# Masks later, fewer tile-mode changes, and the last gate tile in two column halves

## The chip, the cores and the metric

The kernel runs on one core of one Trainium2 chip. The metric is device time in microseconds, the median of seven runs. The profile is that of one execution, taken by the hardware profiler; TensorE is called PE in it, its weight loads PEld, VectorE DVE, ScalarE ACT, GpSimd POOL and SyncE SP. L977 is line 977 of the kernel before.

## The reference, cut to what matters

One sequence of S = 2048 tokens with D = 448 features goes through a linear attention with 16 heads of 28 features and through a squared-ReLU network of F = 1792 hidden units; the second gates the first.

```
xn = layernorm(x)
q, k, v = split(xn @ wqkv)                 # 16 heads of 28
phi(t) = where(t > 0, t + 1, exp(t)) + 1e-6
kv = sum over tokens of phi(k) v^T         # per head, 28 x 28
z  = sum over tokens of phi(k)             # per head, 28
s  = (phi(q) kv / (phi(q) z + 1e-6)) @ wo
g  = silu(relu(xn @ w1 + b1)^2 @ w2 + b2)
out = x + s * g
```

All inputs and the output are bf16.

## The kernel before, in words

The tokens are 16 tiles of 128 (NT); four tiles are a group of 512 (NG = 4). D = 448 is contracted as three chunks of 128 features and a tail of 64. The transposed tile xT holds the tail twice, on partitions 0 to 63 and 64 to 127 (the copies `dup`, L713, and L495 double these columns of xn ahead of the transposition), and the weight tiles hold their 64 tail rows twice as well. So a tail of one product can run on the upper half of the TensorE array while that of another runs on the lower.

A "mode" is how the array is cut into tiles for a matmul: 128x128 (rows x columns) is the whole array, 64x128 two row halves side by side, 128x64 two column halves. The mode follows from the partitions of the operands and of the output.

**Who sets the order.** The kernel is written as a list of operations (`Program.add`), each with its engine, what it reads and writes, and an assumed duration. `schedule()` keeps TensorE and SyncE in the order of the source and lets the other engines choose, by assumed times, the ready operation that is due first. `prio`, `rank` and `hold` change that choice. `emit()` derives the semaphore waits from the reads and writes. An engine executes its list in order, so an operation that waits holds all behind it. `Buf` names a PSUM bank, and eight exist.

**Stages**, in TensorE's order:
1. The start (L1108 to L1145): `warm` issues 43 matmuls on a zero tile. Beside it tiles 0 to 3 are loaded and normalised one by one (`ln_stats`, `ln_rstd`, `ln_norm`, `dup`), and TensorE transposes them (`x_transpose0`, L726; two tiles at a time, evicted by ACT and DVE). The first eight H products (`hh`) are worked off in column halves as the tiles arrive (`pe_part`, L701). `bias_columns` transposes b1 (L780). POOL makes the constants: `ident`, and the masks `hmask`, `zmask` and `ehd` by twelve `affine_select` operations on the memset tiles (`late_constants`, L383).
2. The middle (L1154 to L1182): K, Q and H products of the groups in fours (`quads`, `pe_four`), in 64x128 mode. Later tiles are transposed by DMA. `phi` (L598) evicts K and Q by ACT (exp) and two DVE operations; `h_out` (L670) evicts H by ACT and squares it on DVE or ACT. `qx` (L653) forms the last 64 q features of eight tiles. `zsum` (L628) adds the k tiles on POOL. Four gate tiles (`gg`, L967) are already made here.
3. Attention sums (L1176 to L1181): `token_sum` contracts xn with phi(k) over all tokens; `z_cols` (L840) turns zb, the sum on each partition, into the vector z by five one-column matmuls, and DVE spreads it with `zmask` into zsb; `den` forms phi(q) z.
4. The rest: `spread` brings 1/den to all features with `ehd` and multiplies it into phi(q); `fold_wv` and `fold_wo` form kv wo, with `hmask`. Then gate tiles (`ggs`) alternate with S tiles (`ss4`). A gate tile is 14 matmuls of 448 columns (L977), an addition of b2 on DVE (L994) and a silu on ACT (L1004). An S tile is multiplied by its gate tile on DVE (L1014), x is added on POOL (L1020), and SP issues the output.
5. The end (L1206 to L1219): gate tiles 13 and 14; the tails of S tiles 12 to 15 (`s_tails`, tile 15 as 256 and 192 columns); the other chunks (`s_main`) of tiles 12 and 13; 11 of the 14 matmuls of gate tile 15, led by b2 as a one-row matmul (L975); tile 14; the last three gate matmuls; the two parts of tile 15. Gate tile 15 is read by silu straight from PSUM (L989). Here x is added on DVE. SP waits for all outputs at the very end.

Of the kernel before, what the change touches and what calls it, by code (L numbers as in the profile page):

```python
# [6 lines left out]
ALU = mybir.AluOpType  # L7
AF = mybir.ActivationFunctionType

P = 128  # L10
S, D, F = 2048, 448, 1792
NT, NG, NF = S // 128, S // 512, F // 128
NH, DH = 16, 28
# [281 lines left out]
def bass_recurrent_scan__linear_attn_block__dense_activation_squared_relu__prompt_kernel(  # L295
    nc, A_x, A_wqkv, A_wo, B_x, B_w1, B_b1, B_w2, B_b2, out
):
    with ExitStack() as es:
# [11 lines left out]
        onesr = sb("onesr", [1, P], bf)  # L310
        ehd = sb("ehd", [P, D], bf)
        x_tok = sb("x_tok", [P, NT, D], bf)
        xn = sb("xn", [P, NT, 512], bf)
# [17 lines left out]
        zb = sb("zb", [P, D], bf)  # L331
# [23 lines left out]
        def select(view, name, pattern, base, cm, fill, op=ALU.is_ge, dur=0.3):  # L355
            masks.append(
                add(
                    "pool",
                    lambda e, _: e.affine_select(
                        out=view, in_=view, pattern=pattern, compare_op=op, fill=fill, base=base, channel_multiplier=cm  # L360
                    ),
                    [name], [name], dur,
                )
            )

        masks = []
# [8 lines left out]
        vset(onesr[:, :], 1.0, "onesr")  # L375
        vset(zsb[:, :, :], 0.0, "zsb0")
# [3 lines left out]
        vset(kvm[:, :, :], 0.0, "kvm", dur=1.0)  # L380
        pool(lambda e, _: e.memset(eps6[:, :], 1e-6), ["eps6"], dur=0.1)

        def late_constants():  # L383
            hv = hmask[:, :].rearrange("p (b j) -> p b j", b=HC)
            select(hv, "hmask", [[-DH, HC], [0, DH]], 0, 1, 0.0)
            select(hv, "hmask", [[DH, HC], [0, DH]], DH - 1, -1, 0.0)
            for view, pat, base in (
                (zmask[:, 0:3, :], [[P, 3], [-DH, 32]], 0),
                (zmask[:, 3, :], [[-DH, 32]], 384),
                (zmask[:, 4, :], [[-DH, 32]], 320),  # L390
            ):
                select(view, "zmask", pat, base, 1, 0.0)
                select(view, "zmask", [[-a, n] for a, n in pat], DH - 1 - base, -1, 0.0)
            select(zmask[:, 3, :], "zmask", [[0, 32]], 63, -1, 0.0)
            select(zmask[:, 4, :], "zmask", [[0, 32]], -64, 1, 0.0)
            pool(lambda e, _: e.memset(ones[:, :], 1.0), ["ones"], dur=0.1)
            ev = ehd[:, :].rearrange("p (h j) -> p h j", h=NH)
            for g in range(NG):
                select(ev, "ehd", [[-1, NH], [0, DH]], -32 * g, 1, 1.0, ALU.not_equal, dur=0.6)
# [62 lines left out]
        masks.clear()  # L462
        late_constants()
# [164 lines left out]
        def zsum(i):  # L628
            o = zb if i == NT - 1 else zacc
            add(  # L630
                "pool",
                lambda e, _: e.tensor_tensor(  # L632
                    out=o[:, :], in0=pk[:, 0, :] if i == 1 else zacc[:, :], in1=pk[:, i, :], op=ALU.add
                ),
                [("pk", i), ("pk", 0) if i == 1 else "zacc"], ["zb" if i == NT - 1 else "zacc"], 1.05,
            )

# [15 lines left out]
        def qx(u):  # L653
            b = Buf("QX")

            def f(e, _):
                last = None
                for c in range(4):
                    rw = slice(0, 128) if c < 3 else slice(0, 64)
                    for o in (0, 1):  # L660
                        last = e.matmul(  # L661
                            ps(b)[64 * o : 64 * o + 64, 0:512], w_qkv[rw, c, 384:448],
                            xT[rw, 8 * u + o : 8 * u + 8 : 2, c, :], start=(c == 0), stop=(c == 3),
                        )
                return last

            add("pe", f, xnames(2 * u) + xnames(2 * u + 1) + wnames("wq"), [b], 4 * MM(512) + 0.1)
            phi(b, pqx[:, u, :, :].rearrange("p a b -> p (a b)"), ("pqx", u), 512)
# [171 lines left out]
        def z_cols():  # L840
            b = Buf("Z")

            def f(e, _):
                last = None
                for c in range(3):
                    last = e.matmul(
                        ps(b)[:, c : c + 1], zb[:, c * P : (c + 1) * P], ones[:, :], start=(c == 0), stop=True,
                        skip_group_check=True,
                    )
                for o in (0, 1):  # L850
                    last = e.matmul(
                        ps(b)[64 * o : 64 * o + 64, 3 + o : 4 + o], zb[:, 384:448], ones[:, :], start=False, stop=True,
                        skip_group_check=True,
                    )
                return last

            add("pe", f, ["zb", "ones"], [b], 0.35)
            for v, c0, c1, lo, hi in ((0, 0, 3, 0, 128), (1, 3, 4, 0, 64), (2, 4, 5, 64, 128)):

                def zops(e, _, c0=c0, c1=c1, lo=lo, hi=hi):  # L860
                    z = ps(b)[lo:hi, c0:c1]
                    z = free_ap(z, [[1, c1 - c0], [0, 32]])
                    return e.tensor_tensor(out=zsb[lo:hi, c0:c1, :], in0=z, in1=zmask[lo:hi, c0:c1, :], op=ALU.mult)

                add("dve", zops, [b, "zmask", "zsb0"], [("zsb", v)], 0.2)

# [28 lines left out]
        def den():  # L895
            def f(e, _):
# [19 lines left out]
                [("zsb", v) for v in range(3)] + [("pq", g, c) for g in range(NG) for c in range(3)]  # L916
# [50 lines left out]
        def gg(si, b=None, part=None):  # L967
            b = b or Buf("G")
            g = si // 4
            fis = range(NF) if part is None else part  # L970

            def f(e, _):
                last = None
                if part is not None and fis[0] == 0:
                    last = e.matmul(ps(b)[:, 0:D], onesr[:, :], b2b[0:1, :], start=True, stop=False)  # L975
                for fi in fis:
                    last = e.matmul(  # L977
                        ps(b)[:, 0:D], r2[:, fi, si * P : (si + 1) * P], w_2[:, fi, :],
                        start=(fi == 0 and part is None), stop=(fi == NF - 1),
                    )  # L980
                return last

            rd = [("r2", g, fi) for fi in fis] + ["w2"] + (["b2b", "onesr"] if part is not None else [])
            add("pe", f, rd + ([b] if fis[0] else []), [b], len(fis) * MM(D) + (0.19 if part is not None else 0))
            gs = gbuf[:, si % NGB, :]
            if part is not None:
                if fis[-1] == NF - 1:
                    add(
                        "act", lambda e, _: e.activation(out=gs, in_=ps(b)[:, 0:D], func=AF.Silu), [b, "acts"],  # L989
                        [("g", si % NGB)], 0.576,  # L990
                    )
            else:
                add(
                    "dve", lambda e, _: e.tensor_tensor(out=gs, in0=ps(b)[:, 0:D], in1=b2b[:, :], op=ALU.add),  # L994
                    [b, "b2b"], [("g", si % NGB)], 0.624,
                )
# [11 lines left out]
        def gate(si, b, lo, hi, k, final):  # L1008
            w = hi - lo
            gs, ob = gbuf[:, si % NGB, lo:hi], obuf[:, si % NOB, lo:hi]  # L1010
            nm = ("o", si % NOB)
            wr = [nm] if k is None else [("ol", k)] + ([nm] if lo == 0 else [])
            add(
                "dve", lambda e, _: e.tensor_tensor(out=ob, in0=ps(b)[:, 0:w], in1=gs, op=ALU.mult),  # L1014
                [b, ("g", si % NGB)], wr, 0.1 + w * 0.00118,
            )
            nm = wr[0]
            add(
                "dve" if final else "pool",
                lambda e, _: e.tensor_tensor(out=ob, in0=ob, in1=x_tok[:, si, lo:hi], op=ALU.add),  # L1020
                [nm, ("x", si)], [nm], 0.08 + w * 0.0007 if final else 1.05,
            )
            dma("sp", tok(out, si, si + 1)[:, 0, lo:hi], ob, [("out", si, lo)], P * w * 2, [nm])
# [84 lines left out]
        warm(43, 0.106)  # L1108
# [24 lines left out]
        for op in masks:  # L1133
            op.hold = [t23]
# [15 lines left out]
        ln(4, 8, lead=3, hold=[t23])  # L1150
        load_x(12, 16)
# [17 lines left out]
        gg(3)  # L1169
        quads("H2.8 H2.9 H2.10 H2.11 Q1.1 H2.12 Q1.2 H2.13")  # L1170
# [40 lines left out]
        us = s_tails([(12, 0, D), (13, 0, D), (14, 0, D), (15, 0, 256), (15, 256, D)])  # L1211
        s_main(us[0], 0)
        s_main(us[1], 1)
        gb = Buf("G")
        gg(15, gb, range(0, 11))
        s_main(us[2], 2)
        gg(15, gb, range(11, NF))
        s_main(us[3], 3)
        s_main(us[4], 4)  # L1219
# [30 lines left out]
```

## Time and profile before

| | us |
|---|---|
| median of seven runs | 148.54 (148.14 to 148.94) |
| the profiled execution | 148.76 |
| its span | 147.0 |
| first warm-up matmul starts | 1.05 |
| first transpose starts | 5.80 |
| last matmul starts | 143.40 |
| last output issued | 144.97 |

The profiled execution took 148.76 us; its span, from the first to the last instruction that the profiler recorded, is 147.0, so 1.7 us lie around it. The views used below are: the page's first section (busy time, share of the span and number of instructions of each engine); the chain that ended last, followed back from the end through whatever released each step, as shares and as a list in order of time; the timeline, one row for consecutive instructions of one kind, with the idle time before them and what ended it in brackets; and the DMA issues with their time to landing. [...] consecutive matmuls overlap: the distance between their starts is what one costs.

### The profile page before, as it was taken

What the parts mean: (1) busy time and instruction counts of PE and PEld (TensorE: products, weight loads), DVE (VectorE), ACT (ScalarE), POOL (GpSimd) and SP (SyncE); (2) the same over time, 40 slices, a digit from 0 to 9 for tenths busy, and PEclk for the clock granted to TensorE, in tenths of its full rate; (3) what the DMA queues carried; (4) which work ended last, traced back from release to release, by engine and by line L of the source; (5) the groups of instructions that cost most, each with busy time, mean ns of one, the idle gap of its engine ahead of it and who ended that gap; (6) DMA issues with size and microseconds to landing.
All of it is one profiled execution on the core that took longest, in us unless ns stands there. A gap on an engine that the chain in (4) does not pass through costs nothing.

```text
span 147.0 us, 2838 instructions
## 1 busy us (share of the span) xinstructions
PE 142.2 (97%) x1127; PEld 72.7 (49%) x1127; DVE 97.2 (66%) x222; ACT 79.3 (54%) x152; POOL 34.4 (23%) x50
## 2 busy tenths in 40 slices
PE   7999999999999999999999999999999999999990
PEld 7874555555454444444443554454444545545450
DVE  6979699799987995268999410079674426136343
ACT  3618797988886981388879713897311110310200
POOL 6800025371000551000550000000001908109100
PEclk9999999999999999999999999999999999999999
DMA  3967799933900600000000000000000211102212
GB/s 85 322 224 229 162 236 381 304 102 62 85 0 18 124 4 0 0 0 4 2 0 0 4 0 0 0 7 0 0 0 0 71 58 61 64 0 65 64 62 62
DMA packets 16025, 10.53 MB, mean 72 GB/s; under 512 B 7372, under 2 KB 15628, under 8 KB 16012
## 3 DMA queue, kind: packets, MB, share of 16 engines
q1 hardware_dynamic: 15824, 10.28, 26.8%
q8 instruction: 9, 0.15, 0.5%
q10 hardware_dynamic: 188, 0.07, 0.2%
q14 instruction: 4, 0.03, 0.1%
HBM read 6.94 MB, written 1.84 MB: 60 GB/s over the span
## 4 chain that ended last, share of the span: by engine, by line
PE 94%; ACT 3%; DVE 1%; issue 0%; DVEq 0%
PE pb L977 29%; PE pb L705 25%; PE pb L622 7%; PE pb L793 6%; PE pb L646 6%; PE pb L1031 6%; PE pb L1081 3%; PE pb L701 2%; ACT r L672 2%; PE pb L661 2%; PE pb L1067 1%; PE pb L799 1%; PE pb L878 1%; PE pb L737 1%; PE pb L938 1%; PE pb L822 1%
## 5 line engine op out<-in xcount | busy, mean ns | idle before, releaser
L977 PE MATMUL pb<-w,r 128*128 128x448 bf16 x224 | 44.3, 353 | 0.0
L672 ACT ACTIVATE r<-pb,b1f 128x512 bf16<-128x512 f32 x54 | 33.8, 690 | 10.6 <-PE pb L705 10.6
L705 PE MATMUL pb<-xT,w 64*128 64x512 bf16 (+1 forms) x291 | 38.7, 377 | 0.3 <-ACT r L672 0.3
L977 PEld LDWEIGHTS pb<-w,r 128*128 128x128 bf16 x224 | 21.1, 98 | 21.2 <-issue 2.0
L1004 ACT ACTIVATE gbuf<-gbuf 128x448 bf16<-128x448 bf16 x15 | 8.5, 580 | 29.7 <-DVE gbuf L994 29.7
L632 POOL TENSOR_TENSOR zacc<-zacc,pk 128x448 f32<-128x448 f32 x13 | 14.5, 1114 | 39.9 <-DVE pk L612 35.8
L1020 POOL TENSOR_TENSOR obuf<-obuf,x_tok 128x448 bf16<-128x448 bf16 x12 | 12.0, 1030 | 48.7 <-DVE obuf L1014 48.7
L705 PEld LDWEIGHTS pb<-xT,w 64*128 64x128 bf16 (+1 forms) x291 | 15.0, 94 | 16.2 <-ACT r L672 0.7
L994 DVE TENSOR_TENSOR gbuf<-pb,b2b 128x448 bf16<-128x448 f32 x15 | 9.4, 624 | 16.6 <-PE pb L977 16.5
L686 DVE TENSOR_TENSOR r<-r 128x512 bf16<-128x512 bf16 x35 | 16.6, 512 | 3.0 <-ACT r L672 3.0
L1014 DVE TENSOR_TENSOR obuf<-pb,gbuf 128x448 bf16<-128x448 f32 (+2 forms) x17 | 9.2, 591 | 7.1 <-PE pb L1031 4.7
L622 PE MATMUL pb<-w_qkv,xT 64*128 64x448 bf16 x112 | 13.3, 350 | 0.0
L961 DVE TENSOR_TENSOR pqT<-pqT,pb 128x512 bf16<-128x512 bf16 x12 | 7.4, 680 | 8.6 <-PE pb L938 8.6
L687 ACT ACTIVATE r<-r 128x512 bf16<-128x512 bf16 x21 | 12.6, 634 | 0.0
L646 PE MATMUL pb<-xT,w_qkv 64*128 64x512 bf16 x84 | 11.1, 376 | 0.0
L705 PE MATMUL pb<-xT,w_1r 64*128 64x512 bf16 x56 | 10.5, 377 | 0.0
L612 DVE SCALAR_TENSOR_TENSOR pk<-pb,pk 128x448 bf16<-128x448 f32 x16 | 9.9, 624 | 0.5
L600 ACT ACTIVATE pk<-pb 128x448 bf16<-128x448 f32 x16 | 7.8, 541 | 4.4 <-PE pb L622 4.4
L466 DVE BATCH_NORM_STATS2 st<-x_tok 128x6 f32<-128x448 bf16 x16 | 9.2, 614 | 0.6 <-DMA x_tok<-in_A_x_dram 0.6
L793 PE MATMUL pb<-pk,xn 128*128 128x448 bf16 x48 | 9.4, 353 | 0.0
L622 PEld LDWEIGHTS pb<-w_qkv,xT 64*128 64x128 bf16 x112 | 5.8, 94 | 5.7 <-issue 0.4
L612 DVE SCALAR_TENSOR_TENSOR pqT<-pb,pqT 128x512 bf16<-128x512 f32 x12 | 8.2, 689 | 0.3
(90 smaller groups left out, 129.2 us busy)
## 6 DMA issues: line engine op xcount, KB each, us to landing
out_dram<-obuf SPq DMA_DIRECT2D x15, 112.0 KB, 1.8
w<-in_B_w_dram SPq DMA_DIRECT2D x1, 1568.0 KB, 9.5
x_tok<-in_A_x_dram SPq DMA_DIRECT2D x3, 448.0 KB, 4.0
w<-in_B_w_dram SPq DMA_DIRECT2D x3, 384.0 KB, 4.3
w_qkv<-in_A_wqkv_dram SPq DMA_DIRECT2D x3, 336.0 KB, 4.8
w_o<-in_A_wo_dram SPq DMA_DIRECT2D x1, 392.0 KB, 9.3
w_qkv<-in_A_wqkv_dram SPq DMA_DIRECT2D x6, 56.0 KB, 4.3
x_tok<-in_A_x_dram SPq DMA_DIRECT2D x2, 112.0 KB, 2.1
```

The costliest lines, as they stand in the source:

```text
L612: lambda e, _: e.scalar_tensor_tensor(out=slot, in0=ps(buf)[:, 0:n], scalar=1.0 + 1e-6, in1=slot, op0=ALU.add, op1=ALU.max),
L622: return e.matmul(ps(b)[:, 0:D], xT[rw, si, c, :], w_qkv[rw, c, D : 2 * D], start=start, stop=stop)
L632: lambda e, _: e.tensor_tensor(out=o[:, :], in0=pk[:, 0, :] if i == 1 else zacc[:, :], in1=pk[:, i, :], op=ALU.add),
L646: return e.matmul(ps(b)[:, 0:512], w_qkv[rw, c, m * P : (m + 1) * P], xT[rw, 4 * g : 4 * g + 4, c, :], start=start, stop=stop,)
L672: rl = lambda e, _: e.activation(out=slot, in_=ps(b)[:, 0:512], func=AF.Relu, bias=b1f[:, fi : fi + 1])
L686: return e.tensor_tensor(out=slot, in0=slot, in1=slot, op=ALU.mult)
L687: return e.activation(out=slot, in_=slot, func=AF.Square)
L705: return e.matmul(ps(b)[:, 0:512], lhs, xT[rw, 4 * g : 4 * g + 4, c, :], start=start, stop=stop, skip_group_check=not full,)
L793: last = e.matmul(ps(b)[:, 0:D], xn[:, si, c * P : (c + 1) * P], pk[:, si, :], start=(si == 0), stop=(si == NT - 1),)
L977: last = e.matmul(ps(b)[:, 0:D], r2[:, fi, si * P : (si + 1) * P], w_2[:, fi, :], start=(fi == 0 and part is None), stop=(fi == NF - 1),)
L994: "dve", lambda e, _: e.tensor_tensor(out=gs, in0=ps(b)[:, 0:D], in1=b2b[:, :], op=ALU.add),
L1020: lambda e, _: e.tensor_tensor(out=ob, in0=ob, in1=x_tok[:, si, lo:hi], op=ALU.add),
```

## The change

- **Masks.** `late_constants` is split. `z_masks` is called behind the LayerNorm of tiles 4 to 7, and its selects read the last transposed copy of tiles 2 and 3. `head_masks` (hmask and ehd) is called behind gate tile 3, and its selects read that tile. The small tile `ones` is set at the start as before. The memsets of `onesr` and of zsb go.
- **qx.** The tail chunk is no longer contracted on 64 rows but on all 128, where the features stand twice, with a new weight tile wqh = 0.5 x the doubled weights. DVE makes wqh once, from the loaded q weights, and qx reads it.
- **z_cols.** zb is widened to 512 columns, the last 64 a copy of its features 384 to 447 made by POOL behind the last `zsum`. The five one-column matmuls all use 128 weight columns, and one DVE operation writes all of zsb instead of three.
- **The end.** `s_tails` and the outputs cut tile 15 into 224 and 224 columns. The order is S tiles 12, 13, 14; the left half of gate tile 15 (`gg_part`: b2 by a matmul with `ident`, then 14 of 224 columns, silu of 224 columns from PSUM); the left half of S; the right half of the gate tile; the right half of S.
- **Warm-up.** 40 matmuls instead of 43.

In DVE's new order, wqh stands behind the second ReLU (L677) of the first group and ahead of the two squares (L686) that start at 15.51 in the profile. On POOL, the six head masks stand behind the eleventh `zsum`. TensorE's order is otherwise the same.

```diff
-        zb = sb("zb", [P, D], bf)
+        wqh = sb("wqh", [P, 64], bf)
+        zb = sb("zb", [P, 512], bf)
...
-        vset(onesr[:, :], 1.0, "onesr")
-        vset(zsb[:, :, :], 0.0, "zsb0")
...
-        def late_constants():
+        def z_masks(after):
...
+        def head_masks(after):
...
+            if i == NT - 1:
+                pool(lambda e, _: e.tensor_copy(zb[:, D:512], zb[:, 384:D]), ["zbd"], ["zb"], dur=0.25)
...
-                    rw = slice(0, 128) if c < 3 else slice(0, 64)
                     for o in (0, 1):
                         last = e.matmul(
-                            ps(b)[64 * o : 64 * o + 64, 0:512], w_qkv[rw, c, 384:448],
-                            xT[rw, 8 * u + o : 8 * u + 8 : 2, c, :], start=(c == 0), stop=(c == 3),
+                            ps(b)[64 * o : 64 * o + 64, 0:512], w_qkv[:, c, 384:448] if c < 3 else wqh[:, :],
+                            xT[:, 8 * u + o : 8 * u + 8 : 2, c, :], start=(c == 0), stop=(c == 3),
                         )
...
+            if u == 0:
+                add(
+                    "dve",
+                    lambda e, _: e.tensor_scalar(
+                        out=wqh[:, :], in0=w_qkv[:, 3, 384:448], scalar1=0.5, scalar2=None, op0=ALU.mult
+                    ),
+                    wnames("wq"), ["wqh"], 0.1,
+                )
...
-                for c in range(3):
+                for c in range(5):
+                    k = min(c, 3) * P
                     last = e.matmul(
-                        ps(b)[:, c : c + 1], zb[:, c * P : (c + 1) * P], ones[:, :], start=(c == 0), stop=True,
+                        ps(b)[:, c : c + 1], zb[:, k : k + P], ones[:, :], start=(c == 0), stop=True,
                         skip_group_check=True,
                     )
-                for o in (0, 1):
-                    last = e.matmul(
-                        ps(b)[64 * o : 64 * o + 64, 3 + o : 4 + o], zb[:, 384:448], ones[:, :], start=False, stop=True,
-                        skip_group_check=True,
-                    )
...
+        def gg_part(si, lo, hi):
+            b = Buf("G")
+            w = hi - lo
+
+            def f(e, _):
+                last = e.matmul(ps(b)[:, 0:w], ident[:, :], b2b[:, lo:hi], start=True, stop=False)
+                for fi in range(NF):
+                    last = e.matmul(
+                        ps(b)[:, 0:w], r2[:, fi, si * P : (si + 1) * P], w_2[:, fi, lo:hi], start=False,
+                        stop=(fi == NF - 1),
+                    )
+                return last
+
+            rd = [("r2", si // 4, fi) for fi in range(NF)] + ["w2", "b2b", "ident"]
+            add("pe", f, rd, [b], (NF + 1) * max(MM(w), 0.098))
+            add(
+                "act",
+                lambda e, _: e.activation(out=gbuf[:, si % NGB, lo:hi], in_=ps(b)[:, 0:w], func=AF.Silu),
+                [b, "acts"], [("gh", lo)] + ([("g", si % NGB)] if lo == 0 else []), 0.2 + 0.00084 * w,
+            )
...
-        warm(43, 0.106)
+        warm(40, 0.107)
...
         ln(4, 8, lead=3, hold=[t23])
+        z_masks([("xTp", 2, 3)])
...
         gg(3)
+        head_masks([("g", 3)])
...
-        us = s_tails([(12, 0, D), (13, 0, D), (14, 0, D), (15, 0, 256), (15, 256, D)])
-        s_main(us[0], 0)
-        s_main(us[1], 1)
-        gb = Buf("G")
-        gg(15, gb, range(0, 11))
-        s_main(us[2], 2)
-        gg(15, gb, range(11, NF))
-        s_main(us[3], 3)
-        s_main(us[4], 4)
+        us = s_tails([(12, 0, D), (13, 0, D), (14, 0, D), (15, 0, 224), (15, 224, D)])
+        for k in range(3):
+            s_main(us[k], k)
+        gg_part(15, 0, 224)
+        s_main(us[3], 3)
+        gg_part(15, 224, D)
+        s_main(us[4], 4)
```

## The prediction

> **What bounds the kernel now.** I read the page's busy times first, then the share line of the chain that ended last, then that chain in order of time, and last the timeline of the few places that the change touches.
>
> ```profile
> PE 142.2 (97%) x1127; PEld 72.7 (49%) x1127; DVE 97.2 (66%) x222; ACT 79.3 (54%) x152; POOL 34.4 (23%) x50
> ...
> PE 94%; ACT 3%; DVE 1%; issue 0%; DVEq 0%
> ```
>
> TensorE has work in 97% of the span and is 94% of the chain. So an edit pays in one of three ways: it takes time out of TensorE's stream, it shortens what runs before TensorE has its data (the first 6 us), or what runs after its last matmul (the last 4 us). Work of other engines in between is worth nothing until it makes TensorE wait. The chain by time (start us, duration us, what) shows all places:
>
> ```profile
> 1.05 4.71 PE pb L1081 x43
> 5.76 0.11 PE pb L780
> 5.87 0.70 PE pb L737 x8
> ...
> 38.05 1.10 PE pb L661 x8
> ...
> 86.90 0.05 PE pb L846 x3
> 86.95 0.12 PE pb L851 x2
> 87.08 3.13 PE pb L793 x16
> ...
> 97.24 2.65 PE pb L977 x14
> ...
> 104.85 2.75 PE pb L977 x14
> ...
> 139.45 0.29 PE pb L975
> 139.74 2.19 PE pb L977 x11
> ...
> 143.10 0.55 ACT gbuf L989
> 143.68 0.69 DVE obuf L1014 x2
> 144.37 0.20 DVE obuf L1020
> ```
>
> Price of one tile-mode change: the 14 matmuls of a gate tile take 2.65 us behind another full-array group (97.24; 0.189 us each) and 2.75 us behind a group of 32-row tiles (104.85): 0.10 us. The eight matmuls of qx (L661) take 1.10 us where eight q matmuls in one mode take 0.86 us elsewhere in the chain: two changes, 0.12 us each. So 0.10 to 0.12 us a change, and it is TensorE's own time.
>
> **Part 1, mode changes.** qx before runs six matmuls as 128x64 tiles, then two as 64x64; with wqh all eight are 128x64. One change less, twice in the kernel: 2 x 0.11 = 0.22 us (bounds 0.20 and 0.24). z_cols before is three full matmuls, two of 128x64, and back to full: 0.05 + 0.12 us and the surplus of the 16 after it (3.13 against 16 x 0.189 = 3.03), together 0.27. After, five full ones: 0.05 for three and about 0.03 for each further one, 0.11. Saved 0.16 us; if a one-column matmul with a 128-column weight cost 0.06 each, as the 16 at L822 do (0.96 us), still 0.05. I take 0.15.
>
> These edits hang work on other engines. zb's copied columns are one small POOL copy behind the last zsum, which ends at 75.9 us, 10.8 us ahead of z_cols: nothing. Three DVE operations on zsb become one; den reads it 3 us later: nothing. wqh is a new DVE operation with a new wait, for the three loads of the q weights, and in DVE's order it stands ahead of two squares:
>
> ```profile
> 15.51 0.75 DVE L686 TENSOR_TENSOR r<-r 128x512 bf16<-128x512 bf16 x2
> 17.42 0.28 DVE L605 TENSOR_SCALAR pk<-pk 128x448 bf16<-128x448 bf16 x1 [1.16 <-ACT pk L600]
> ```
>
> The last of the loads is issued at 12.56 and takes 3.8 us, so it lands at 16.4. DVE then holds the two squares from 15.5 to 16.4, runs wqh (0.1 to 0.2) and the squares (0.75) and is free at 17.3 to 17.4. Its next work waits for ScalarE until 17.42 anyway. The idle 1.16 us covers it, with 0.1 us to spare. Without that cover, the pk operations behind it, and then the PSUM banks of the k tiles, would come free later, up to 0.2 us; TensorE has no wait there now, so I put it at 0, bounds 0 and +0.1.
>
> **Part 2, masks.** Before, POOL cuts twelve masks from 1.6 to 7.6 us, beside the LayerNorm chain of the first tiles:
>
> ```profile
> 3.82 3.17 POOL L359 TENSOR_SCALAR_AFFINE_SELECT ehd<-ehd 128x448 bf16<-128x448 bf16 x4
> ...
> 4.84 0.53 DVE L722 COPY xn<-xn 128x64 bf16<-128x64 bf16 x1
> ...
> 5.27 0.38 DVE L486 TENSOR_SCALAR xn<-x_tok,mv,rstd 128x448 bf16<-128x448 bf16 x1
> ...
> 7.89 0.18 DVE L722 COPY xn<-xn 128x64 bf16<-128x64 bf16 x1
> ```
>
> The same copy takes 0.18 us once POOL is quiet (7.89) and 0.53 at 4.84; it ends at 5.37, just behind the select that POOL ran from 4.62 to 5.33. So POOL's select held it. With the masks elsewhere the copy ends about 5.02 and the second normalisation starts when its rstd is there (ScalarE's row 4.89, 0.20: so 5.13) instead of 5.27. At its usual 0.38 it ends near 5.51, and the transposes can start at 5.56 to 5.58; before, they started at 5.80. The two memsets of zsb and onesr (0.1 to 0.2 us on DVE) were hidden: DVE waits 0.26 us for x at 2.96 anyway.
>
> The transposes at 5.80 were not only late for that: the 43 warm-up matmuls (0.107 each) ended there. Forty end 0.32 us earlier, at about 5.5 with the bias transpose. So trimming and masks only pay together, and the later of the two decides: 0.22 us, bounds 0 (the copy stays slow) and 0.32 (the whole trim). What is late next: the w1 block of the first H matmuls lands at 6.5 (issued 2.19, 4.3 us), 0.3 us before L701 starts at 6.79; its first matmul would then start at 6.57. The shift fits, just. Behind that DVE, ScalarE and TensorE follow one another in a chain with no slack until 15.2, so the 0.22 carries on.
>
> Here a rule speaks against the trim. The Trainium skill ("TensorE: Matmul & The Clock Gate", Part 1) says that the array runs at half rate until it has been busy through about one free-running window of 3.4 us. The trace agrees on the half rate (0.107 us per 128-column warm-up matmul, 0.056 per transpose from 5.87 on), and shows the release near 5.6, though the granted clock is printed as 1.00 throughout. By the row nothing is lost, since the release comes as the transposes start; by the rule a pause before the release could cost a second window. I take the row, as the pause is about 0.1 us, and keep the rule as the rival that ends slower.
>
> Where the masks go: the eight zmask selects (2.3 us) wait for the copy of xTp (2,3), so run from 10.3 to 12.6, beside statistics, which took 0.61 us with or without POOL, and end before the normalisations at 13.4. The four of ehd and two of hmask (3.8 us) wait for the fourth gate tile, which DVE adds at 58.8, so run to 63.3. POOL's next zsum starts at 69.6, DVE is idle for 2.58 us up to 62.0, and ehd and hmask are read behind 95. At worst two squares there are held 0.5 us, and nobody reads them for 40 us: 0.
>
> **Part 3, the end.** Before: the bias row as a one-row matmul (a change in, a change out: 0.29 + 2.19 against 12 x 0.189 = 2.27, 0.21 us too much), 14 gate matmuls, the two parts of the last S tile. Then a chain behind TensorE: silu of 448 columns, two multiplies, two adds, and an issue at 144.97 that is followed by 1.6 us to landing and 0.5 us to the end.
>
> After: 9 S matmuls from 138.14 (9 x 0.19, to 139.85), 15 gate matmuls of 224 columns, 3 of S, 15, 3. Spacing is linear in the columns (0.189 at 448; the six last, three of 256 and three of 192, start from 142.90 to 143.40: 0.109 and 0.083), so 0.096 at 224. Left half done at 141.29, S at 141.58, right half at 143.02, S at 143.31: the stream ends 0.17 us earlier than 143.48 (0.21 of mode changes, less 0.04 for 15 more instructions). The last gate matmul starts at 142.93 and is out 0.26 later, 143.19 (before 143.06). Silu +0.04; 224 columns cost about 0.35 (448 took 0.54; exp rows of 448 and 512 differ by 0.9 ns a column), to 143.57. Multiply +0.03, 0.385 (0.42 at 256, 0.35 at 192): 143.99. Add +0.03, 0.27: 144.29. Issue 144.32. All of the left half is over before 142.7 and its issue does not stand in front. Against 144.97: 0.65 us.
>
> A rule speaks against this too: the same page, section "LDWEIGHTS", gives columns / 1.2 ns, so 107 ns for 128 columns. Were that the pace, 30 narrow matmuls at 0.107 instead of 0.096 would cost 0.33 us. The row says no: with 192 columns, each with its own 128x128 load, they start every 0.083 us, and transposes every 0.056. I take the row; the rule makes the end 0.32 instead of 0.65.
>
> **The sum.** 0.22 + 0.15 + 0.22 + 0.65 = 1.24 us. The profiled execution took 148.76 us (span 147.0, 1.7 around it), so 147.52; it lies 0.22 above the median of the seven runs, 148.54, which gives 147.3.
>
> **The rivals.**
> - The start gives nothing: the copy is slow for another reason, or the first weights land later, and TensorE idles through the trimmed 0.32. For: the slack of w1 is 0.3 us. Against: the copy ends with POOL's select. 148.54 - 1.02 = 147.5.
> - The halves are paced by weight loads: 147.3 + 0.33 = 147.65. Against: the 0.083 row.
> - Slower: the pause before the clock's release costs another half-rate window. Place: 5.6 to 9.0 us, where TensorE is busy for 3.1 us (18 matmuls of 0.109, 16 transposes, 4 warm-ups); doubled, less what DVE hides, about +2 us: 147.5 + 2 = 149.5. It decides as soon as the 0.1 us of idle counts as a quiet window. Against: 4.5 of the first 4.6 us stay busy.
> - Slower too, by DVE held at wqh, needs the q weights 2 us later than they landed.
>
> **How the numbers follow.** All parts pay, 147.3: 0.66. No gain at the start, 147.5: 0.14. Weight-bound halves, 147.65: 0.08. Clock released late, 149.5: 0.07. Another new stall that eats it all: 0.05. 0.3% is 0.45 us, about what a measurement of this kernel can tell from no change: faster is below 148.1. The first three nearly all fall there: faster 0.82, same 0.09, slower 0.09. Range: all bounds good give 148.54 - (0.24 + 0.16 + 0.32 + 0.65) = 147.2; all bounds bad, weight-bound halves among them, 148.54 - (0.20 + 0.05 + 0 + 0.32) + 0.1 for DVE = 148.1. Below I add 0.3 for the runs' own spread (148.14 to 148.94): 146.9 to 148.1; the two slow cases, 0.12, lie outside.
>
> **What would show it.** The copy of dup at 0.18 and transposes near 5.58; qx 0.98 us in the chain; L793 behind z_cols at 3.03; the last output's issue near 143.7 (144.32 less the 0.59 won before it); gate matmuls every 0.096. Wrong if warm-up spacing of 0.107 goes on into L701, if DVE shows a wait on w_qkv beyond 17.4, or if silu of 224 columns takes nearly 0.54.

## The result and the profile after

| | before | after |
|---|---|---|
| median, us | 148.54 (148.12 to 149.29, 31 runs) | 147.24 (146.86 to 147.93, 12 runs) |
| profiled execution, us | 148.76 | 147.93 |
| its span, us | 147.0 | 146.2 |

The ratio is 0.9915, with a 95% interval of 0.9898 to 0.9933: 1.3 us faster. The prediction was 147.3. The profiled execution is the longest of the twelve, and its span is only 0.8 us shorter than that of before; why is part of what follows.

The page of the changed kernel, busy times and shares of the chain that ended last:

```profile
PE 141.2 (97%) x1139; PEld 73.7 (50%) x1139; DVE 96.9 (66%) x219; ACT 79.5 (54%) x153; POOL 35.3 (24%) x51
...
PE 89%; DMA 5%; DVE 2%; ACT 1%; SPq 1%; issue 0%
```

TensorE still bounds it, with 1.0 us less work. New are two DMA transfers in the chain. The chain in order of time (start us, us, what):

```profile
1.26 2.88 DMA x_tok<-in_A_x_dram
...
5.61 0.41 DVE xn L481
...
6.06 0.52 PE pb L741 x6
...
11.01 4.35 DMA w_1r<-in_B_w_dram
15.36 0.09 issue
15.45 1.04 PE pb L709 x8
...
38.30 0.98 PE pb L657 x8
...
86.91 0.10 PE pb L851 x5
87.02 3.05 PE pb L797 x16
...
139.97 1.34 PE pb L992 x14
...
143.08 0.37 ACT gbuf L1002
...
143.47 0.40 DVE obuf L1022
...
143.89 0.28 DVE obuf L1028
```

qx takes 0.98 us instead of 1.10. z_cols and the 16 matmuls behind it take 0.10 + 3.05 instead of 0.05 + 0.12 + 3.13. At the end, silu, multiply and add are 0.37, 0.40 and 0.28 us, one each. The first lines are not what was forecast: the transposes (L741) start at 6.06, later than the 5.80 of before, behind the load of the second x tile, which lands at 4.14. The timeline of DVE there (the bracket is idle time ahead of the instruction, and what ended it):

```profile
4.16 0.63 DVE L461 BATCH_NORM_STATS2 st<-x_tok 128x6 f32<-128x448 bf16 x1 [0.40 <-DMA x_tok<-in_A_x_dram]
...
5.33 0.18 DVE L726 COPY xn<-xn 128x64 bf16<-128x64 bf16 x1
5.61 0.40 DVE L481 TENSOR_SCALAR xn<-x_tok,mv,rstd 128x448 bf16<-128x448 bf16 x1
```

The copy takes 0.18 us, as forecast. But DVE waits for the second tile, issued at 1.26 as before, for 2.9 us instead of 2.1. So the masks helped and a load cost more, in the same execution.

The other load in the chain, w_1r, explains most of why this execution is the longest. TensorE waits 0.32 us for it and goes on at 15.45, 0.09 us behind its landing. The wait is not new. In the profile before it is 0.33 us:

```profile
15.20 0.82 PE L705 MATMUL pb<-xT,w 64*128 64x512 bf16 x6 [0.33 <-ACT r L672]
```

The bracket names ScalarE, but the same load landed at 15.11, again 0.09 us earlier; and in e9, the changed kernel once more, TensorE goes on at 14.92, while the same ScalarE operation ends at 15.41. So the load is what is waited for. The wait also stands in e1 and e11 and in none of the other nine profiles: from the first K matmul to the first Q matmul it is 5.99 to 6.16 us with it and 5.67 without. The profile of e9 starts its transposes within 0.05 us of this one, has no such wait, and its span is 0.55 us shorter, of which 0.48 us is this wait.

The wait that wqh adds, in the same timeline later:

```profile
16.57 0.18 DVE L666 TENSOR_SCALAR wqh<-w_qkv 128x64 bf16<-128x64 bf16 x1 [0.72 <-DMA w_qkv<-in_A_wqkv_dram]
16.66 0.75 DVE L690 TENSOR_TENSOR r<-r 128x512 bf16<-128x512 bf16 x2
17.67 0.28 DVE L600 TENSOR_SCALAR pk<-pk 128x448 bf16<-128x448 bf16 x1 [0.25 <-ACT pk L595]
```

DVE waits 0.72 us for the q weights, and is done with the squares 0.25 us before ScalarE lets it go on. The cover held.

### The profile page after: what moved, and what is told of

Its sections match the earlier page's. It is cut to its first block, busy times and chain, and to the rows that moved or that the text cites. A ratio compares the mean times of both kernels' runs of the same rounds, so it can differ in the third digit from the quotient of the medians.

```text
span 146.2 us, 2861 instructions
## 1 busy us (share of the span) xinstructions
PE 141.2 (97%) x1139; PEld 73.7 (50%) x1139; DVE 96.9 (66%) x219; ACT 79.5 (54%) x153; POOL 35.3 (24%) x51
## 4 chain that ended last, share of the span: by engine, by line
PE 89%; DMA 5%; DVE 2%; ACT 1%; SPq 1%; issue 0%
PE pb L970 28%; PE pb L709 25%; PE pb L617 7%; PE pb L797 6%; PE pb L643 6%; PE pb L1039 6%; DMA w_1r<-in_B_w_dram 3%; DMA x_tok<-in_A_x_dram 2%; PE pb L992 2%; PE pb L705 1%; PE pb L1075 1%; PE pb L657 1%; PE pb L803 1%; PE pb L874 1%; SPq L401 1%; PE pb L741 1%
## 5 line engine op out<-in xcount | busy, mean ns | idle before, releaser
L970 PE MATMUL pb<-w,r 128*128 128x448 bf16 x210 | 41.3, 353 | 0.0
L970 PEld LDWEIGHTS pb<-w,r 128*128 128x128 bf16 x210 | 19.8, 98 | 20.0 <-issue 1.5
L1022 DVE TENSOR_TENSOR obuf<-pb,gbuf 128x448 bf16<-128x448 f32 (+1 forms) x17 | 9.2, 592 | 6.6 <-PE pb L1039 4.7
```

What stands on the lines that cost most here:

```text
L970: last = e.matmul(ps(b)[:, 0:D], r2[:, fi, si * P : (si + 1) * P], w_2[:, fi, :], start=(fi == 0), stop=(fi == NF - 1),)
```

## The experiments

Each kernel was timed against the kernel before on its chip; "less" is the difference of the two medians. The ratio is taken over all executions, so it is not the quotient of the two medians.

| kernel | median, us | before, us | less, us | ratio (95% interval) |
|---|---|---|---|---|
| e1 end only | 147.94 | 148.64 | 0.70 | 0.9947 (0.9923 to 0.9970) |
| e2 modes only | 148.25 | 148.64 | 0.39 | 0.9974 (0.9950 to 0.9999) |
| e3 masks only | 148.42 | 148.64 | 0.22 | 0.9988 (0.9964 to 1.0011) |
| e4 masks, 40 warm-ups | 148.41 | 148.64 | 0.23 | 0.9978 (0.9958 to 0.9998) |
| e5 after, 43 warm-ups | 147.09 | 148.37 | 1.28 | 0.9913 (0.9891 to 0.9935) |
| e6 after, 30 warm-ups | 147.11 | 148.37 | 1.26 | 0.9931 (0.9900 to 0.9961) |
| e7 after, cut at 320 | 147.06 | 148.37 | 1.31 | 0.9908 (0.9880 to 0.9936) |
| e8 after, second x tile from ScalarE's queue | 147.46 | 148.37 | 0.91 | 0.9931 (0.9912 to 0.9950) |
| e9 after, again | 147.33 | 148.80 | 1.47 | 0.9912 (0.9882 to 0.9941) |
| e10 after, masks early | 147.87 | 148.80 | 0.93 | 0.9956 (0.9929 to 0.9983) |
| e11 after, cut at 320, 43 warm-ups | 147.14 | 148.80 | 1.66 | 0.9895 (0.9869 to 0.9922) |

The intervals are 0.3 to 0.45 us wide each way. So the medians bear on the large parts, and the traces must tell the small ones.

**e1, the end alone.** The kernel before with the last group of the change:

```diff
+        us = s_tails([(12, 0, D), (13, 0, D), (14, 0, D), (15, 0, 224), (15, 224, D)])
+        for k in range(3):
+            s_main(us[k], k)
+        gg_part(15, 0, 224)
+        s_main(us[3], 3)
+        gg_part(15, 224, D)
+        s_main(us[4], 4)
```

> The kernel before with the end alone changed (gate tile 15 and S tile 15 in halves of 224 columns, bias by the identity). Theory (the parts add up, each by its own term): 0.65 us less, so 147.9 where before has 148.54, with the last issue 6.2 us after the first S matmul of the end instead of 6.8. Rival (the start gains nothing, as the profile of the changed kernel, in which the second x tile landed at 4.14 us instead of 3.40, suggests; the end then must bring more than its term): 0.9 to 1.0 us less, so 147.6. Weight-bound halves would show 147.9 + 0.3.

0.70 us less. Its chain:

```profile
138.42 1.81 PE pb L1079 x9
140.23 0.10 PE pb L994
140.32 1.34 PE pb L996 x14
...
143.43 0.37 ACT gbuf L1006
...
143.81 0.40 DVE obuf L1026
...
144.24 0.28 DVE obuf L1032
```

14 matmuls of 224 columns, each with its own weight load, in 1.34 us are 0.096 each (the timeline prints 0.26 for one, so they overlap), the bias one 0.10 in the same mode. What this fixes is the distance from the last of the five S tails to the last output's issue: 7.00 us before, 6.38 in e1 and in every other kernel with the halves, and the output lands 1.52 us later instead of 1.59. 0.62 + 0.07 = 0.69 us. The theory holds, and no pace of 0.107 us by weight loads is seen.

**e2, the modes alone.** The kernel before with wqh, the wider zb, the five full one-column matmuls and the single zsb operation:

```diff
+                            ps(b)[64 * o : 64 * o + 64, 0:512], w_qkv[:, c, 384:448] if c < 3 else wqh[:, :],
...
-                for c in range(3):
+                for c in range(5):
```

> The kernel before with the mode changes alone (qx with wqh, z_cols with five full matmuls, zb widened, one zsb operation). Theory: 0.37 us less (0.22 from qx, 0.15 from z_cols), 148.15, with qx at 0.98 us in the chain. Rival (DVE held at wqh costs TensorE time): 148.5.

0.39 us less. qx takes 0.98 us twice in its chain and z_cols 0.10. This profile is of its longest execution, and DVE's timeline shows the wait of wqh at its worst:

```profile
17.45 0.18 DVE L671 TENSOR_SCALAR wqh<-w_qkv 128x64 bf16<-128x64 bf16 x1 [1.18 <-DMA w_qkv<-in_A_wqkv_dram]
17.54 0.75 DVE L695 TENSOR_TENSOR r<-r 128x512 bf16<-128x512 bf16 x2
18.21 0.27 DVE L605 TENSOR_SCALAR pk<-pk 128x448 bf16<-128x448 bf16 x1
```

Here the cover is used up: the pk operation follows with no idle time. TensorE still runs on until 24 us (there it waits 0.6 us, for a reason that e3 shares, see the last section). So the rival, DVE held at wqh at TensorE's cost, is not seen even then. In five of the nine profiles with wqh (e2, e5, e8, e9, e10) the pk operation follows without idle time, and in none does TensorE wait between 15.5 and 23.5 us.

**e3 and e4, the start in two steps.** e3 is the kernel before with the masks moved:

```diff
-        masks.clear()
-        late_constants()
...
+        z_masks([("xTp", 2, 3)])
...
+        head_masks([("g", 3)])
```

e4 adds the trim:

```diff
-        warm(43, 0.106)
+        warm(40, 0.107)
```

> The kernel before with the masks moved and still 43 warm-up matmuls. Theory (warm-up and LayerNorm chain end together, the later one decides): 0 to 0.1 us less, since the transposes still wait for the warm-up; the copy of dup takes 0.18 us instead of 0.53. Rival (POOL's masks alone held the start): 0.2 us less. Rival (the second x tile's landing decides): no change in the median, with the landing in the trace moving the transposes.

> The kernel before with the masks moved and 40 warm-up matmuls: the whole start. Theory: 0.22 us less, 148.3, transposes near 5.58 when the second x tile lands by 3.4. Rival (the second x tile's landing decides, and it can be 4.1): no gain in the median, 148.5, transposes at landing + 1.9 us. Rival (the clock's release comes late): 150.

0.22 and 0.23 us less. By the medians masks alone bring as much as masks and trim; by the ratios it is 0.2 and 0.3 us. With intervals of 0.3 us and more the times do not settle whether "they only pay together" (the interval of e3 reaches over 1). The traces must. In the profile of e3 it looked as forecast, the transposes standing behind the warm-up:

```profile
4.84 0.18 DVE L718 COPY xn<-xn 128x64 bf16<-128x64 bf16 x1
...
5.12 0.40 DVE L482 TENSOR_SCALAR xn<-x_tok,mv,rstd 128x448 bf16<-128x448 bf16 x1
...
5.87 1.03 PE L733 MATMUL pb<-ident,xn 128*128 128x128 bf16 x8
```

The normalised tile is there at 5.52, the transposes start at 5.87. But this is one kind of execution. Two things differ from one execution to the next, and put beside each other the profiles show them (us; "fast from" is where matmuls of 128 columns go from 0.107 to 0.056 us apart):

| kernel | masks | warm-ups | second x tile lands | copy of dup | transposes | after landing | fast from |
|---|---|---|---|---|---|---|---|
| before | early | 43 | 3.40 | 0.53 | 5.80 | 2.40 | 5.5 to 5.8 |
| e1 | early | 43 | 3.33 | 0.53 | 5.87 | 2.54 | 7.0 |
| e2 | early | 43 | 4.09 | 0.68 | 6.48 | 2.39 | 3.8 |
| e10 | early | 40 | 3.89 | 0.68 | 6.33 | 2.44 | 5.0 |
| e3 | moved | 43 | 3.43 | 0.18 | 5.87 | 2.44 | 6.9 |
| e5 | moved | 43 | 3.32 | 0.18 | 5.58 | 2.26 | 4.9 |
| e7 | moved | 40 | 3.39 | 0.18 | 5.63 | 2.24 | 6.7 |
| e4 | moved | 40 | 4.02 | 0.18 | 5.94 | 1.92 | 4.4 |
| after | moved | 40 | 4.14 | 0.18 | 6.06 | 1.92 | 5.1 |
| e9 | moved | 40 | 4.09 | 0.18 | 6.01 | 1.92 | 4.4 |
| e11 | moved | 43 | 4.17 | 0.18 | 6.09 | 1.92 | 5.1 |

With the tile late (about 4.1), TensorE is long done with the warm-up, 40 or 43, and the masks alone decide: 1.92 us from landing to transposes instead of 2.4, 0.5 us. With the tile early (about 3.4), the warm-up counts only if the array stays at half rate to its end, as in e3 (5.87); if it turns fast before, 43 matmuls end early enough (e5, 5.58, the place that was forecast for 40). So "they only pay together" falls: it holds in one kind of execution. (With the tile early, DVE takes up its statistics only behind those of the first tile, at 3.7, so the distance from landing is longer.)

A late end of the half rate costs time of its own, with 43 warm-ups and with 40: from the first transpose to the first H product it is 1.30 us in e1, e3 and e7 (fast from 6.7 to 7.0), and 0.98 to 0.99 in the other eight of the table.

**e5 and e6, the warm-up in the changed kernel**, with `warm(43, 0.107)` and `warm(30, 0.107)`.

> The changed kernel with 43 warm-up matmuls again. Theory (the transposes wait for the later of the warm-up and the second x tile, which lands near 3.4 in some executions and near 4.1 in others; with 4.1 the trim is worth nothing, with 3.4 up to 0.3): 0.1 to 0.2 us above the changed kernel's 147.24, so 147.35 to 147.45. Rival (the trim itself is the gain of the start): 0.32 above, 147.55. Rival (the trim is worth nothing): 147.24.

1.28 us less than before where the changed kernel had 1.30: no worth of the trim is seen. With intervals of 0.3 us, a worth of 0.32 is unlikely and one of 0.1 is not excluded.

> The changed kernel with 30 warm-up matmuls, so that TensorE pauses for about 1.3 us before the transposes. Theory (the array's half rate ends at a moment of the chip's own, between 4 and 7 us in the profiles so far, if TensorE was busy before; a pause of 1 us near it does little): within 0.3 us of 147.24 in the median, with wider spread. Rival (by the rule of the Trainium skill, a busy window of 3.4 us is needed, and 30 matmuls at 0.107 us fill only 3.2): warm spacing of 0.107 goes on into the first H products, 148 to 149.5.

The median hardly moves, but the twelve executions fall into two groups: eight from 146.89 to 147.23, four from 148.35 to 148.56. The profile caught one of the four. Its chain:

```profile
5.54 1.03 PE pb L741 x8
6.57 0.43 PE pb L1089 x4
7.00 3.41 PE pb L705 x18
```

In the changed kernel the same 18 matmuls took 2.14 us. They go on 0.213 us apart until 9.80 and are 0.109 apart from there, while the granted clock is printed as 1.00 all the time. TensorE had ended its warm-up at 4.4, when it was not yet fast, and but for the small bias transposition paused to 5.54. So the slower rival is real, with its place and its sign; its price is 1.4 us (148.4 less 147.0), not 2, and somewhere between 40 and 30 warm-up matmuls it begins to occur. None of the 18 executions of the changed kernel (first measurement and e9) reached 148. Pauses behind the release, as of 0.85 us in e9 and 1.49 in e2, cost nothing: the transposes behind them start at full rate. The rule of the Trainium skill ("TensorE: Matmul & The Clock Gate", Part 1: full rate after about one busy window of 3.4 us, free-running) fits these runs only in part. A window that runs free of the kernel would fit the spread of the table, 2.7 to 5.9 us behind the first matmul at 1.05. But e2 turned fast after 2.7 us, less than a window, and eight of the twelve executions here kept the short time although 30 matmuls at 0.107 us fill only 3.2. What decides in a single execution stays open.

**e7 and e11, an uneven cut.** 320 and 128 columns instead of 224 and 224, e11 with 43 warm-ups as well:

```diff
-        us = s_tails([(12, 0, D), (13, 0, D), (14, 0, D), (15, 0, 224), (15, 224, D)])
+        us = s_tails([(12, 0, D), (13, 0, D), (14, 0, D), (15, 0, 320), (15, 320, D)])
```

> The changed kernel with the last tile cut into 320 and 128 columns instead of 224 and 224. Theory (what follows TensorE's last gate matmul is paid per column: silu 0.09, multiply 0.12, add 0.05 us less for 96 columns, against 0.08 later gate matmuls, and 128-column matmuls start every 0.056 us as the transposes do): 0.18 us below 147.24, so 147.05. Rival (weight loads pace the narrow matmuls at 0.1 us): 14 x 0.045 = 0.6 us later, so 147.7.

> The changed kernel with the last tile cut into 320 and 128 columns and 43 warm-up matmuls. Theory: 0.23 us below the changed kernel from the end (from the first S tail of the last group to the last issue 6.23 instead of 6.38, landing 1.44 instead of 1.52), nothing from the warm-up. Rival (three warm-up matmuls cost 0.1 to 0.3 when the second x tile is early): 0 to 0.1 below.

The chain of e7:

```profile
139.41 1.90 PE pb L992 x14
...
141.77 0.80 PE pb L992 x14
...
142.59 0.29 ACT gbuf L1002
...
142.90 0.30 DVE obuf L1022
...
143.22 0.23 DVE obuf L1028
```

14 matmuls of 128 columns, each with its own weight load, in 0.80 us: 0.057 each. Silu, multiply and add cost 0.29, 0.30 and 0.23 instead of 0.37, 0.40 and 0.28. From the last S tail to the last issue it is 6.23 us instead of 6.38, and the output lands 1.44 later instead of 1.52: 0.23 us shorter, in both kernels. The medians agree in sign only: e11 is 0.19 below e9, beside it, and e7 gains 1.31 where the changed kernel had 1.30. e11 has the lowest ratio, 0.9895; its interval overlaps that of the changed kernel, so a better version is likely and not shown by the times.

**e8, the second x tile from ScalarE's queue**, in the changed kernel:

```diff
         load_x(0, 1)
-        load_x(1, 2)
+        load_x(1, 2, "act")
         load_x(2, 4)
```

> The changed kernel with the second x tile loaded from ScalarE's queue at 0.84 us instead of second on SP's at 1.26. Theory (its landing sets the start): it lands near 3 to 3.4 always, transposes near 5.55, 0.2 us below 147.24 in the median and less spread, so 147.0. Rival (b1 and the w1 tails, now 0.6 us later on that queue, or the first tile's share of the DMA engines, take it back): 147.24 or more.

The rival won: 0.91 us less than before, so some 0.4 us worse than the changed kernel in the median (the intervals overlap), though the spread is small (147.29 to 147.61). In the profile the tile lands at 3.49, but the first tile lands at 3.27 instead of 2.90, and the transposes start at 5.91. Then TensorE has a gap ahead of the first H product:

```profile
5.91 0.62 PE L741 MATMUL pb<-ident,xn 128*128 128x128 bf16 x8 [0.81 <-DVE xn L481]
6.37 0.39 PE L1089 MATMUL pb<-wz 128*128 128x128 bf16 x4
7.30 0.38 PE L705 MATMUL pb<-xT,w 128*128 128x256 bf16 x2 [0.54 <-ACT vep L470]
```

The engine named in the bracket is not an input of this product. The w1 blocks are: they take 5.7 us to land (median of two) instead of 4.4, the first at 7.17. The tile that came earlier made other loads later.

**e9 and e10, the masks taken back in the changed kernel.** e9 is the changed kernel itself, the measure for the others; e10 takes the reads away that make the selects wait:

```diff
-        z_masks([("xTp", 2, 3)])
+        z_masks([])
...
-        head_masks([("g", 3)])
+        head_masks([])
```

> The changed kernel itself, unaltered, as the measure for the two beside it: 1.3 us below before, as in its first measurement.

> The changed kernel with its mask selects free to run at the start again (their reads of the later tiles taken away), still 40 warm-up matmuls. Theory (moving the masks is what the start gained, the trim added nothing, as 43 warm-up matmuls in the changed kernel cost nothing): 0.2 us above the changed kernel, the copy of dup at 0.5 us or more. Rival (trim and masks each bring a part): 0.1 us above. Rival (neither brings anything, only which executions fell together): no difference, although the copy is slow.

0.54 us above e9 in the median; the intervals overlap slightly. The timeline says how. e10:

```profile
4.47 2.32 POOL L357 TENSOR_SCALAR_AFFINE_SELECT ehd<-ehd 128x448 bf16<-128x448 bf16 x3
...
4.68 0.60 DVE L481 TENSOR_SCALAR xn<-x_tok,mv,rstd 128x448 bf16<-128x448 bf16 x1
...
5.31 0.68 DVE L726 COPY xn<-xn 128x64 bf16<-128x64 bf16 x1
...
5.89 0.38 DVE L481 TENSOR_SCALAR xn<-x_tok,mv,rstd 128x448 bf16<-128x448 bf16 x1
```

Beside POOL's selects the copy of 64 columns takes 0.68 us, where it takes 0.18 in e9, and the normalisation of the first tile 0.60 instead of 0.36. The transposes come 2.44 us after the tile instead of 1.92. The theory holds in sign and cause; its price is 0.5 us in this execution with a late tile, not 0.2.

## Why the prediction was right, and where it was not

- **qx:** 0.22 forecast. From the first q matmul to the first of the token sums it is 60.56 us before and 60.31 to 60.33 in the eight profiles of the changed kernel and its variants: 0.23 to 0.25. Right.
- **z_cols:** 0.15 forecast. From the first of the token sums to the last S tail: 57.30 before, 57.12 to 57.13 in the changed kernel. 0.17. Right.
- **The end:** 0.65 forecast up to the issue of the last output, 0.62 measured; 0.69 with its earlier landing, 0.07, which was left out, and 0.70 in the median of e1. Right.
- **wqh, zb, zsb and the late masks:** put at nothing, and nothing is seen. The selects at 59.7 to 63.9 stretched squares beside them (one took 0.63 us, where before each took 0.42 to 0.43), but the idle time between them took that up: the last three need 1.58 us before (to 64.15) and after (to 64.28).
- **The start:** 0.22 forecast, and 0.22 and 0.23 measured in e3 and e4. The size is right, but with intervals of 0.3 us that is partly luck, and the step is not. It said that "trimming and masks only pay together, and the later of the two decides". With all 43 matmuls the transposes of e5 start at 5.58, and e11's come 1.92 us after the tile as with 40; no worth of the trim is seen in the medians. It also took the landing of the second tile, 3.4 us in one profile, for a constant. It is 3.3 to 3.5 or 3.9 to 4.2. In the second case the masks pay 0.5 us and the trim nothing, and transposes near 5.58 are out of reach, as in the profile after. That the 0.22 carries on was right for another reason than the one given: what TensorE waited for at 15.2 was the w_1r load and not ScalarE, but that load is issued later or earlier with the start (10.75 us before, 11.01 after, the transposes at 5.80 and 6.06).
- **The slower rival:** right in kind, and its full price, 1.4 us, is absent at 40 warm-ups. The pause was not 0.1 us but 0.59 in the profile after and 0.85 in e9, in both behind the release.
- **The weight-load rival:** narrow matmuls started every 0.096 us at 224 columns and every 0.057 at 128 (e7), so the row of the profile was the right choice.

The parts alone sum to 0.70 + 0.39 + 0.23 = 1.32 us, the whole is 1.30. Each is known to about 0.3 us, so the close agreement is partly luck; the traces bear 0.25 + 0.17 + 0.69 = 1.11 of it and leave 0.2 to the start. No sign is seen that the parts get in each other's way. What stays open: whether the trim pays in executions in which the array turns fast late (e7 started its transposes 0.24 us before e3 then, in one profile each), why the second tile lands at two different times, and why the w_1r load takes 4.2 to 4.4 us in four profiles and 3.3 to 3.8 in the others.

## What to carry to other kernels

Cut the last tile so that what follows the last matmul is short: silu, multiply, add and output are paid per column, narrow matmuls of TensorE cost in proportion to their columns down to 128, and the gain stood in every profile with the halves, since nothing runs behind it that could hide it. A helper engine's idle work is not free when it lies beside another engine's short copies; bind it by a real dependency, since an order in a schedule alone does not make an engine wait (the kernel before puts the masks behind the transposition of tiles 2 and 3 by `hold`, and POOL ran them from 1.56 us). And read the start of a kernel from several profiles before calling one row the bound; compare the time at which a wait ends with the landings of loads, since a bracket can name the wrong engine.

## What the runs showed of the hardware that was not expected

- The array's half rate ended between 3.8 and 7.0 us in the eleven profiles of the table, and at 9.80 in e6; the granted clock was printed as 1.00 in these stretches.
- The second x tile, a load of 112 KB issued at 1.26, took 2.1 to 2.3 us to land in six profiles and 2.6 to 2.9 in six (e8 issues it elsewhere). Together with the late end of the half rate (0.3 us) and the waits at 15 us (which cost 0.3 to 0.5) and 24 us (0.6 to 0.7) it accounts for differences between executions of one kernel of the size seen; which of them fell together in an execution that was not profiled is not known.
- In the profiles of e2 and e3, with the longest executions, TensorE waits for a k tile's PSUM bank near 24 us (e2's waits, in total us, times, longest us):

```profile
PE pb L622 <- DVE pk L612: 0.6, 1, 0.6
```

DVE stood before that at the statistics of x tiles 8 to 11, which landed at 21.9 and 21.5 instead of 19.5 in the profile before. It occurs with wqh (e2) and without (e3), so wqh is not its cause; why the load is late is open.
